# Computing the first chunk's hidden layer in two 256-row halves, with half of x transposed by the DMA

## The chip, the cores and the metric

The kernel runs on one core of a Trainium2 chip. The metric is the device time of one execution in microseconds (us); lower is better. The profile's span is about 1.8 us shorter than that time.

## The reference

Forward and backward of a two-layer block with SiLU in between, all in bfloat16; x and grad_out are 2048 x 640, w1 is 640 x 1536, w2 is 1536 x 640.

```python
def _fwd_reference(x, w1, w2):
    h = jnp.einsum("bsd,df->bsf", x, w1)
    h = _silu(h)
    out = jnp.einsum("bsf,fd->bsd", h, w2)
    return out
# reference: out, and the gradients of x, w1, w2 for a given grad_out
```

## The kernel before

The 2048 rows are processed in four chunks of 512. For a chunk the kernel computes h (w1 stationary, x transposed as moving operand), then the out product, then the gradients. The first chunk differs from the others: at the start nothing is loaded, so its x is transposed on TensorE, and h, the out product, the g matmuls and the gradient of x follow one another. All loads go into one DMA queue, in program order. While the first load is under way, 36 matmuls on zeros keep TensorE busy ("warm"), so that its clock comes up.

```python
        warm = cpool.tile([P, P], dt_in, name="warm")
        nc.vector.memset(warm[:], 0.0)
        warm_a = cpool.tile([P, 1], FP32, name="warm_a")
        nc.scalar.activation(warm_a[:], warm[:, 0:1], ACT.Silu)
        wp = ps_h.tile([P, SC], FP32, name="wp", tag="hp")
        for i in range(NWARM):
            nc.tensor.matmul(wp[:, 0:P], lhsT=warm[:], rhs=warm[:], start=True, stop=True)
        # ... identity, weight tiles, load_xT and load_goT (DMA transposes of 512 rows)

        def pe_xT(c, halves):
            xT = xpool.tile([P, DT, SC], dt_in, name="xT")
            nst = STC // halves
            for hh in range(halves):
                for dt_ in range(DT):
                    tp = ps_h.tile([P, nst, P], dt_in, name="tp", tag="hp")
                    for j in range(nst):
                        st = c * STC + hh * nst + j
                        nc.tensor.transpose(tp[:, j, :], x_nat[:, st, dt_ * P:(dt_ + 1) * P], ident[:])
                    dst = xT[:, dt_, hh * nst * P:(hh + 1) * nst * P]
                    if dt_ % 2 == 0:
                        nc.vector.tensor_copy(out=dst, in_=tp[:].rearrange("p j q -> p (j q)"))
                    else:
                        nc.scalar.copy(out=dst, in_=tp[:].rearrange("p j q -> p (j q)"))
            return xT

        FH = FC // 2
        nc.sync.dma_start(out=x_nat[:, 0:STC, :], in_=x_v[:, 0:STC, :])
        nc.sync.dma_start(out=w1_nat[:, :, 0:FH], in_=w1_v[:, :, 0:FH])
        nc.sync.dma_start(out=w1_nat[:, :, FH:FC], in_=w1_v[:, :, FH:FC])
        for fc in range(1, NFC):
            nc.sync.dma_start(out=w1_nat[:, :, fc * FC:(fc + 1) * FC], in_=w1_v[:, :, fc * FC:(fc + 1) * FC])
        for hf in range(2):
            nc.sync.dma_start(out=w2_nat[:, :, hf * DH:(hf + 1) * DH], in_=w2_v[:, :, hf * DH:(hf + 1) * DH])
        goT_next = load_goT(0)
        for fc in range(NFC):
            nc.sync.dma_start_transpose(out=w2T[:, :, fc * FC:(fc + 1) * FC], in_=w2[fc * FC:(fc + 1) * FC, :])
        nc.sync.dma_start_transpose(out=w1T[:], in_=w1[:, :])

        xT_next = pe_xT(0, 1)

        def h_group(ft, xT, aT, ghT):
            hp = ps_h.tile([P, SC], FP32, name="hp")
            for dt_ in range(DT):
                nc.tensor.matmul(
                    hp[:],
                    lhsT=w1_nat[:, dt_, ft * P:(ft + 1) * P],
                    rhs=xT[:, dt_, :],
                    start=(dt_ == 0),
                    stop=(dt_ == DT - 1),
                )
            nc.scalar.activation(aT[:, ft, :], hp[:], ACT.Silu)
            t = tpool.tile([P, SC], FP32, name="t")
            nc.scalar.activation(t[:], hp[:], ACT.Tanh, scale=0.5)
            v = tpool.tile([P, SC], dt_in, name="v")
            nc.vector.tensor_scalar(out=v[:], in0=t[:], scalar1=-0.5, scalar2=0.5, op0=ALU.mult, op1=ALU.add)
            nc.vector.scalar_tensor_tensor(
                out=ghT[:, ft, :], in0=aT[:, ft, :], scalar=1.0, in1=v[:], op0=ALU.subtract, op1=ALU.mult
            )

        # ... g_group: the same for grad_out and w2T

        def sd_phase(c, lhs_all, rhs_all, dst_v, on_act):
            o_sb = opool.tile([P, STC, D], dt_in, name="o_sb")
            for sl in range(STC):
                op_ = ps_o.tile([P, 2, 512], FP32, name="op")
                for ft in range(FT):
                    for hf in range(2):
                        nc.tensor.matmul(
                            op_[:, hf, 0:DH],
                            lhsT=lhs_all[:, ft, sl * P:(sl + 1) * P],
                            rhs=rhs_all[:, ft, hf * DH:(hf + 1) * DH],
                            start=(ft == 0),
                            stop=(ft == FT - 1),
                        )
                # ... copy out of PSUM, store

        for c in range(NCH):
            # ... next chunk's transposes
            if c == 0:
                for ft in range(FT):
                    h_group(ft, xT, aT, ghT)
                nc.sync.dma_start(
                    out=aT_scr[:, c * SC:(c + 1) * SC].rearrange("(ft p) s -> p ft s", p=P), in_=aT[:]
                )
                sd_phase(c, aT, w2_nat, out_v, True)
                for ft in range(FT):
                    g_group(ft, goT, ghT)
                # ... ghT to memory, gradient of x
                continue
            # ... chunks 1 to 3: h and g groups alternate
```

## Time and profile before

| | |
|---|---|
| time, first three runs (us) | 323.03 median, 323.01 to 323.51 |
| span of the profiled run | 321.2 |
| TensorE busy | 316.2 (98%) |
| first h matmul starts | 6.35 |
| first matmul of the out product starts | 19.30 |
| second half of w2 has landed | 18.60 |

Two parts of the page of the kernel before: its first line, and the chain of work that ended last, by engine.

```profile
span 321.2 us, 4386 instructions
...
## 4 chain that ended last, share of the span: by engine, by line
PE 97%; DMA 1%; issue 0%; DVE 0%; DVEq 0%
```

TensorE (PE) is nearly the whole chain. What it does not own is the head, which the timeline of TensorE shows. The columns are start and length in us, engine, line, operation, what it writes and reads, the shapes, the count, and in brackets the idle time before and what ended it.

```profile
0.99 3.81 PE L90 MATMUL wp<-warm 128*128 128x128 bf16 x36 [0.99 <-DVE warm L85]
5.06 1.30 PE L118 MATMUL tp<-ident,x_nat 128*128 128x128 bf16 x20 [0.26 <-DMA x_nat<-in_x_dram]
6.35 13.11 PE L144 MATMUL hp<-xT,w_nat 128*128 128x512 bf16 x58
19.30 13.20 PE L180 MATMUL op<-w_nat,aT 128*128 128x320 bf16 x96
```

The transposes begin when x has landed, h follows at once, the out product follows h at once. So this head is made of one wait (x) and then pure TensorE work: the 12.95 us from 6.35 to 19.30 are 60 matmuls at 216 ns (two of the 60 records are missing from the trace). To start h sooner is the only way to shorten it, and it pays only while nothing else becomes the last to arrive.

The same view of the queue that issues the loads:

```profile
0.74 0.43 SPq L127 DMA_DIRECT2D x_nat<-in_x_dram  x1
1.24 0.49 SPq L128 DMA_DIRECT2D w_nat<-in_w_dram  x1
1.77 0.52 SPq L129 DMA_DIRECT2D w_nat<-in_w_dram  x1
2.34 2.36 SPq L131 DMA_DIRECT2D w_nat<-in_w_dram  x2
4.74 4.92 SPq L133 DMA_DIRECT2D w_nat<-in_w_dram  x2
9.70 9.09 SPq L107 DMA_TRANSPOSE goT<-in_grad_out_dram  x1
```

L127 is x, L128 to L131 are the four pieces of w1, L133 the two halves of w2, L107 the first DMA transpose. These are issue times. When a load has landed is in the trace's landing records (the last of the load's 16 completions): x 5.01, w1's pieces 6.08, 7.15, 9.30 and 11.21, w2's halves 14.79 and 18.60. The out product uses both halves of w2 from its second matmul on, so w2 has 0.7 us of room: 18.60 against 19.30.

### The profile page before, as it was taken

The numbers are of one execution on the slowest core, as the hardware profiler recorded it, in microseconds if no ns is written. First come the engines' busy times: TensorE is split into PE (matmuls) and PEld (weight loads), VectorE is DVE, ScalarE is ACT, GpSimd is POOL, SyncE is SP. The second block draws the span as 40 slices with busy tenths as digits, with TensorE's granted clock in tenths as the row PEclk, the third lists the DMA queues.
The fourth block names the chain that finished last, engine by engine and source line by source line (L and its number), as shares of the span: only waits on it lengthen the run. The fifth ranks groups of instructions, "written<-read, shape, count | busy, mean of one in ns | idle before, by whom it ended". The sixth has DMA issues, their size and how long they took to land.

```text
span 321.2 us, 4386 instructions
## 1 busy us (share of the span) xinstructions
PE 316.2 (98%) x1926; PEld 188.5 (59%) x1944; DVE 99.1 (31%) x172; ACT 78.9 (25%) x136; POOL 0.7 (0%) x6
## 2 busy tenths in 40 slices
PE   8999999999999999999999999999999999999996
PEld 6467457544577644477754467777777775444443
DVE  1860553577501287800357740220000000110001
ACT  3961000455210155411044521001111111000100
POOL 0000000000000000000000000000000000000000
PEclk9999999999999999999999999999999999999999
DMA  7999999998794020291020079909999996211111
GB/s 235 318 191 200 220 274 241 363 289 274 213 290 137 6 78 0 78 316 67 17 82 0 0 254 245 239 17 236 226 218 213 266 219 211 85 38 44 35 42 41
DMA packets 113731, 52.32 MB, mean 163 GB/s; under 512 B 84144, under 2 KB 113712, under 8 KB 113712
## 3 DMA queue, kind: packets, MB, share of 16 engines
q1 hardware_dynamic: 113712, 52.04, 64.1%
q8 instruction: 15, 0.25, 0.3%
q14 instruction: 4, 0.03, 0.0%
HBM read 9.18 MB, written 21.76 MB: 96 GB/s over the span
## 4 chain that ended last, share of the span: by engine, by line
PE 97%; DMA 1%; issue 0%; DVE 0%; DVEq 0%
PE op L180 32%; PE op L263 16%; PE hp L163 16%; PE hp L144 16%; PE hp L302 15%; DMA x_nat<-in_x_dram 1%; PE hp L284 1%; PE tp L118 0%; DVE g_2755 L295 0%; DVEq L295 0%
## 5 line engine op out<-in xcount | busy, mean ns | idle before, releaser
L144 PE MATMUL hp<-xT,w_nat 128*128 128x512 bf16 x229 | 56.3, 379 | 0.6
L163 PE MATMUL hp<-goT,w2T 128*128 128x512 bf16 x238 | 56.8, 379 | 0.1
L180 PE MATMUL op<-w1T,ghT 128*128 128x320 bf16 x384 | 52.8, 299 | 0.0
L180 PE MATMUL op<-w_nat,aT 128*128 128x320 bf16 x384 | 52.8, 299 | 0.0
L263 PE MATMUL op<-go_nat,a_blk 128*128 128x320 bf16 x384 | 52.3, 299 | 0.0
L151 ACT ACTIVATE aT<-hp 128x512 bf16<-128x512 f32 x48 | 28.7, 597 | 83.0 <-PE hp L144 83.0
L302 PE MATMUL hp<-gh_blk,x_nat 128*128 128x512 bf16 x219 | 48.2, 379 | 0.3
L180 PEld LDWEIGHTS <-aT 128*128 128x128 bf16 x384 | 37.5, 98 | 15.3
L180 PEld LDWEIGHTS <-ghT 128*128 128x128 bf16 x384 | 37.5, 98 | 14.8
L263 PEld LDWEIGHTS <-a_blk 128*128 128x128 bf16 x384 | 37.5, 98 | 14.7
L163 PEld LDWEIGHTS <-w2T 128*128 128x128 bf16 x240 | 23.5, 98 | 28.2
L144 PEld LDWEIGHTS <-w_nat 128*128 128x128 bf16 x240 | 23.4, 98 | 27.8
L170 DVE SCALAR_TENSOR_TENSOR ghT<-ghT,hp 128x512 bf16<-128x512 bf16 x48 | 32.5, 682 | 16.2 <-PE hp L163 16.2
L191 DVE CAST o_sb<-op 128x640 bf16<-128x640 f32 x16 | 13.2, 825 | 78.6 <-PE op L180 78.6
L302 PEld LDWEIGHTS <-x_nat 128*128 128x128 bf16 x224 | 21.9, 98 | 26.3
L156 DVE SCALAR_TENSOR_TENSOR ghT<-aT,v 128x512 bf16<-128x512 bf16 x48 | 33.0, 687 | 0.6
L153 ACT ACTIVATE t<-hp 128x512 f32<-128x512 f32 x48 | 28.4, 592 | 0.0
L155 DVE TENSOR_SCALAR v<-t 128x512 bf16<-128x512 f32 x48 | 20.5, 427 | 20.5 <-ACT t L153 20.5
L189 ACT ACTIVATE o_sb<-op 128x640 bf16<-128x640 f32 x16 | 11.2, 703 | 49.1 <-PE op L180 49.1
L270 ACT ACTIVATE gw_sb<-op 128x640 bf16<-128x640 f32 x12 | 8.4, 704 | 56.8 <-PE op L263 56.8
L313 DVE CAST g_2475<-hp 128x512 bf16<-128x512 f32 x1 | 0.7, 690 | 58.2 <-PE hp L302 58.2
L90 PE MATMUL wp<-warm 128*128 128x128 bf16 x36 | 3.8, 304 | 1.0 <-DVE warm L85 1.0
(31 smaller groups left out, 26.2 us busy)
## 6 DMA issues: line engine op xcount, KB each, us to landing
aT_scr<-aT SPq DMA_DIRECT2D x4, 1536.0 KB, 6.3
ghT_scr<-ghT SPq DMA_DIRECT2D x4, 1536.0 KB, 9.6
out_dram<-o_sb SPq DMA_DIRECT2D x8, 640.0 KB, 4.4
x_nat<-in_x_dram SPq DMA_DIRECT2D x4, 640.0 KB, 5.4
go_nat<-in_grad_out_dram SPq DMA_DIRECT2D x4, 640.0 KB, 7.0
w_nat<-in_w_dram SPq DMA_DIRECT2D x2, 960.0 KB, 11.5
out_dram<-gw_sb SPq DMA_DIRECT2D x1, 1920.0 KB, 6.9
w_nat<-in_w_dram SPq DMA_DIRECT2D x2, 640.0 KB, 7.6
```

The lines of the kernel that those rows point to most:

```text
L144: nc.tensor.matmul(hp[:], lhsT=w1_nat[:, dt_, ft * P:(ft + 1) * P], rhs=xT[:, dt_, :], start=(dt_ == 0), stop=(dt_ == DT - 1),)
L151: nc.scalar.activation(aT[:, ft, :], hp[:], ACT.Silu)
L153: nc.scalar.activation(t[:], hp[:], ACT.Tanh, scale=0.5)
L155: nc.vector.tensor_scalar(out=v[:], in0=t[:], scalar1=-0.5, scalar2=0.5, op0=ALU.mult, op1=ALU.add)
L156: nc.vector.scalar_tensor_tensor(out=ghT[:, ft, :], in0=aT[:, ft, :], scalar=1.0, in1=v[:], op0=ALU.subtract, op1=ALU.mult)
L163: nc.tensor.matmul(gp[:], lhsT=w2T[:, dt_, ft * P:(ft + 1) * P], rhs=goT[:, dt_, :], start=(dt_ == 0), stop=(dt_ == DT - 1),)
L170: nc.vector.scalar_tensor_tensor(out=ghT[:, ft, :], in0=ghT[:, ft, :], scalar=1.0, in1=gp[:], op0=ALU.add, op1=ALU.mult)
L180: nc.tensor.matmul(op_[:, hf, 0:DH], lhsT=lhs_all[:, ft, sl * P:(sl + 1) * P], rhs=rhs_all[:, ft, hf * DH:(hf + 1) * DH], start=(ft == 0), ...
L189: nc.scalar.activation(dst, op_[:, :, 0:DH], ACT.Copy)
L191: nc.vector.tensor_copy(out=dst, in_=op_[:, :, 0:DH])
L263: nc.tensor.matmul(op_[:, hf, 0:DH], lhsT=a_blk[:, st, :], rhs=go_nat[:, st, hf * DH:(hf + 1) * DH], start=(st == 0), stop=(st == ST - 1),)
L302: nc.tensor.matmul(gp[:], lhsT=x_nat[:, st, dt_ * P:(dt_ + 1) * P], rhs=gh_blk[:, st, :], start=(st == 0), stop=(st == ST - 1),)
```

## The change

The intent is to start h sooner. Of the first 512 rows of x only 256 are loaded and transposed on TensorE; they come as two loads on two issuing engines. w1 comes in six pieces of 256 columns, so that the first piece follows quickly. h of the first chunk is computed in two halves of 256 rows, two blocks of 128 columns of w1 sharing a PSUM bank, so that the ScalarE and VectorE instructions behind it still handle 512 elements each. The second 256 rows come by a DMA transpose, queued behind w1 and ahead of w2. The warm matmuls go from 36 to 25 plus 4. The compiled order puts those 4 ahead of the transposes, so PE runs 29 of them at a stretch.

```diff
-    NWARM = 36
+    NWARM = 25
+    NFILL = 4
 ...
-        nc.sync.dma_start(out=x_nat[:, 0:STC, :], in_=x_v[:, 0:STC, :])
-        nc.sync.dma_start(out=w1_nat[:, :, 0:FH], in_=w1_v[:, :, 0:FH])
-        nc.sync.dma_start(out=w1_nat[:, :, FH:FC], in_=w1_v[:, :, FH:FC])
-        for fc in range(1, NFC):
-            nc.sync.dma_start(out=w1_nat[:, :, fc * FC:(fc + 1) * FC], in_=w1_v[:, :, fc * FC:(fc + 1) * FC])
+        XH = SC // 2
+        NXH = XH // P
+        xT_next = xpool.tile([P, DT, SC], dt_in, name="xT")
+        nc.sync.dma_start(out=x_nat[:, 0, :], in_=x_v[:, 0, :])
+        nc.scalar.dma_start(out=x_nat[:, 1, :], in_=x_v[:, 1, :])
+        for fp in range(F // XH):
+            nc.sync.dma_start(
+                out=w1_nat[:, :, fp * XH:(fp + 1) * XH], in_=w1_v[:, :, fp * XH:(fp + 1) * XH]
+            )
+        nc.scalar.activation(warm_a[:], warm[:, 0:1], ACT.Silu)
+        nc.sync.dma_start_transpose(out=xT_next[:, :, XH:SC], in_=x2[XH:SC, :])
         for hf in range(2):
             nc.sync.dma_start(out=w2_nat[:, :, hf * DH:(hf + 1) * DH], in_=w2_v[:, :, hf * DH:(hf + 1) * DH])
         goT_next = load_goT(0)
 ...
-        xT_next = pe_xT(0, 1)
+        DS = 3
+        for st in range(NXH):
+            tp = ps_o.tile([P, 2, 8, P], dt_in, name="tp", tag="op")
+            for dt_ in range(DT):
+                b, q = (0, dt_) if dt_ < DS else (1, dt_ - DS)
+                nc.tensor.transpose(tp[:, b, q, :], x_nat[:, st, dt_ * P:(dt_ + 1) * P], ident[:])
+            nc.vector.tensor_copy(out=xT_next[:, 0:DS, st * P:(st + 1) * P], in_=tp[:, 0, 0:DS, :])
+            nc.scalar.copy(out=xT_next[:, DS:DT, st * P:(st + 1) * P], in_=tp[:, 1, 0:DT - DS, :])
+        for i in range(NFILL):
+            nc.tensor.matmul(wp[:, 0:P], lhsT=warm[:], rhs=warm[:], start=True, stop=True)
 ...
+        def h_pair(ft, half, xT, aT, ghT):
+            lo, hi = half * XH, (half + 1) * XH
+            hp = ps_h.tile([P, SC], FP32, name="hp")
+            for g in range(2):
+                h_mm(hp[:, g * XH:(g + 1) * XH], ft + g, xT, lo, hi)
+            h_tail(hp[:].rearrange("p (g s) -> p g s", g=2), aT[:, ft:ft + 2, lo:hi], ghT[:, ft:ft + 2, lo:hi])
 ...
             if c == 0:
-                for ft in range(FT):
-                    h_group(ft, xT, aT, ghT)
+                for half in range(2):
+                    for ft in range(0, FT, 2):
+                        h_pair(ft, half, xT, aT, ghT)
```

(Cut: h_mm and h_tail, which hold h_group's matmuls and its four ScalarE and VectorE instructions, and the late load of the 256 rows of x that the weight gradient needs.)

More of the change, by code (lines that the diff above doesn't have):

```diff
@@ L86 @@
         warm_a = cpool.tile([P, 1], FP32, name="warm_a")
-        nc.scalar.activation(warm_a[:], warm[:, 0:1], ACT.Silu)
         wp = ps_h.tile([P, SC], FP32, name="wp", tag="hp")
@@ L108, in load_goT @@
             return goT
-        def pe_xT(c, halves):
-            xT = xpool.tile([P, DT, SC], dt_in, name="xT")
-            nst = STC // halves
-            for hh in range(halves):
-                for dt_ in range(DT):
-                    tp = ps_h.tile([P, nst, P], dt_in, name="tp", tag="hp")
-                    for j in range(nst):
-                        st = c * STC + hh * nst + j
-                        nc.tensor.transpose(tp[:, j, :], x_nat[:, st, dt_ * P:(dt_ + 1) * P], ident[:])
-                    dst = xT[:, dt_, hh * nst * P:(hh + 1) * nst * P]
-                    if dt_ % 2 == 0:
-                        nc.vector.tensor_copy(out=dst, in_=tp[:].rearrange("p j q -> p (j q)"))
-                    else:
-                        nc.scalar.copy(out=dst, in_=tp[:].rearrange("p j q -> p (j q)"))
-            return xT
-        FH = FC // 2
-        nc.sync.dma_start(out=x_nat[:, 0:STC, :], in_=x_v[:, 0:STC, :])
-        nc.sync.dma_start(out=w1_nat[:, :, 0:FH], in_=w1_v[:, :, 0:FH])
-        nc.sync.dma_start(out=w1_nat[:, :, FH:FC], in_=w1_v[:, :, FH:FC])
-        for fc in range(1, NFC):
-            nc.sync.dma_start(out=w1_nat[:, :, fc * FC:(fc + 1) * FC], in_=w1_v[:, :, fc * FC:(fc + 1) * FC])
+        XH = SC // 2
[9 more added lines that the diff above has]
+        nc.sync.dma_start_transpose(out=xT_next[:, :, XH:SC], in_=x2[XH:SC, :])
         for hf in range(2):
@@ L137, with h_tail, h_mm @@
         nc.sync.dma_start_transpose(out=w1T[:], in_=w1[:, :])
-        xT_next = pe_xT(0, 1)
-        def h_group(ft, xT, aT, ghT):
-            hp = ps_h.tile([P, SC], FP32, name="hp")
+        DS = 3
[8 more added lines that the diff above has]
+            nc.tensor.matmul(wp[:, 0:P], lhsT=warm[:], rhs=warm[:], start=True, stop=True)
+        def h_tail(hp, a_out, gh_out):
+            nc.scalar.activation(a_out, hp, ACT.Silu)
+            t = tpool.tile([P, SC], FP32, name="t")
+            nc.scalar.activation(t[:], hp, ACT.Tanh, scale=0.5)
+            v = tpool.tile([P, SC], dt_in, name="v")
+            nc.vector.tensor_scalar(out=v[:], in0=t[:], scalar1=-0.5, scalar2=0.5, op0=ALU.mult, op1=ALU.add)
+            vv = v[:] if len(a_out.shape) == 2 else v[:].rearrange("p (g s) -> p g s", g=a_out.shape[1])
+            nc.vector.scalar_tensor_tensor(
+                out=gh_out, in0=a_out, scalar=1.0, in1=vv, op0=ALU.subtract, op1=ALU.mult
+            )
+        def h_mm(hp, ft, xT, lo, hi):
             for dt_ in range(DT):
                 nc.tensor.matmul(
-                    hp[:],
+                    hp,
                     lhsT=w1_nat[:, dt_, ft * P:(ft + 1) * P],
-                    rhs=xT[:, dt_, :],
+                    rhs=xT[:, dt_, lo:hi],
                     start=(dt_ == 0),
@@ L150, in h_group @@
                 )
-            nc.scalar.activation(aT[:, ft, :], hp[:], ACT.Silu)
-            t = tpool.tile([P, SC], FP32, name="t")
-            nc.scalar.activation(t[:], hp[:], ACT.Tanh, scale=0.5)
-            v = tpool.tile([P, SC], dt_in, name="v")
-            nc.vector.tensor_scalar(out=v[:], in0=t[:], scalar1=-0.5, scalar2=0.5, op0=ALU.mult, op1=ALU.add)
-            nc.vector.scalar_tensor_tensor(
-                out=ghT[:, ft, :], in0=aT[:, ft, :], scalar=1.0, in1=v[:], op0=ALU.subtract, op1=ALU.mult
-            )
+        def h_group(ft, xT, aT, ghT):
+            hp = ps_h.tile([P, SC], FP32, name="hp")
+            h_mm(hp[:], ft, xT, 0, SC)
+            h_tail(hp[:], aT[:, ft, :], ghT[:, ft, :])
+        def h_pair(ft, half, xT, aT, ghT):
+            lo, hi = half * XH, (half + 1) * XH
+            hp = ps_h.tile([P, SC], FP32, name="hp")
+            for g in range(2):
+                h_mm(hp[:, g * XH:(g + 1) * XH], ft + g, xT, lo, hi)
+            h_tail(hp[:].rearrange("p (g s) -> p g s", g=2), aT[:, ft:ft + 2, lo:hi], ghT[:, ft:ft + 2, lo:hi])
         def g_group(ft, goT, ghT):
@@ L205 @@
             if c == 2:
+                nc.sync.dma_start(out=x_nat[:, NXH:STC, :], in_=x_v[:, NXH:STC, :])
                 for j in range(STC, ST, STC):
```

## The prediction

> **What bounds the kernel now.** TensorE: the page has PE busy 98% of a 321.2 us span and 97% of the chain that ended last. Only the head is decided by something else: the chain starts with 4.26 us of waiting for the load of x (issued 0.74, landed 5.01), then 20 transposes (5.06 to 6.35), then h. From the first h matmul (6.35, one 0.2 us gap) to the first matmul of the out product (19.30) PE runs a 512-column matmul every 216 ns (timeline). So the change can win only the head.
>
> **What it wins.** Before h, only 320 KB of x and 320 KB of w1 must land. In the packet records of before, 640 KB had moved by about 4.3 us, the slowest engine landing at 5.0. The 29 warm matmuls at 107 ns end near 4.1; ten transposes instead of twenty save 0.6; the copies end about 5.2. I expect the first h matmul at 5.2 to 5.3, 1.0 to 1.1 us earlier. The clock should be full by then: the Trainium skill ("TensorE: Matmul & The Clock Gate", Part 1) says about 3.4 us of activity lift it; this trace agrees: warm matmuls go from 107 to 55 ns apart at 4.3 us. 120 matmuls of 256 columns should take 108 ns each, 12.96 us like 60 of 512: transposes with a weight load each run 55 ns apart, so loads stay hidden. ACT and DVE instructions keep their 512 elements and cost.
>
> **What it adds, and why the win is lost.** Rows 256 to 511 now come by a DMA transpose queued behind all of w1, and w2 behind that.
> 1. Half 0 of h ends about 11.8 us (6 x 1.08). w1 at 290 to 310 KB/us (its 512-byte packets) is moved by about 9.8. In before the first DMA transpose (goT) began with a stall: its first packets, from 16.5 on, all ended at 18.4, when the last engine had finished w2. Engine spread at the end of w1 is 0.9 us (landings 10.3 to 11.2). So: wait to 10.7, 1.15 us of data (283 KB/us), 0.6 to landing: about 12.5; PE waits 0.7 us. The 16 KB instruction fetch at 15.2, near PE's 194th instruction, moves to about 11.4 and may delay one engine by 1 us more.
> 2. The out product needs both halves of w2; the second landed at 18.6, only 0.7 us ahead of its use. Now it follows a transpose that holds the queue about 2 us where 1 us of x is saved: about 19.6 (18.9 to 20.4). PE, done with h at 19 to 20, starts the out product at about 19.7 instead of 19.30.
> Later loads (goT landed 21.9, needed 32.5; w1T 40.3, needed 45.5) have room for 2 us.
>
> **Prediction.** The head's 1 us is handed back; net +0.4 us: 323.4 us, range 322.3 to 324.6. Chances: faster by over 2% 0.01, within 0.98, slower 0.01.
>
> **What will show it.** First h matmul near 5.25; 256-column matmuls 108 ns apart; a PE gap of 0.5 to 1.5 us between the halves, ended by the DMA of xT; w2's second half landing 18.9 to 20.4 with a PE wait before the out product; later phases unchanged (13.04 us per 96 out matmuls).
>
> **What would make it wrong.** xT landing by 11.8 and w2 by 18.3: then about 322.0. The clock lifted late because of the shorter warm-up: 1 to 3 us worse. w1 pieces falling behind PE.

## The result, and the profile after

The changed kernel took 323.76 us (median of 4 runs, 323.27 to 324.10); the kernel before, in the same rounds, 323.27 (323.01 to 323.70). The ratio is 1.0013, 95% interval 0.9992 to 1.0033: the same.

The page of the changed kernel, the same two parts:

```profile
span 321.5 us, 4496 instructions
...
## 4 chain that ended last, share of the span: by engine, by line
PE 93%; DMA 3%; SPq 3%; issue 0%; DVE 0%; DVEq 0%
```

TensorE has lost 4% of the chain to the DMA and to the queue that issues it (SPq, the queue of SyncE). The chain in order of time shows where (start, length, what):

```profile
5.76 3.52 SPq L120
9.28 0.05 issue
9.33 0.57 SPq L122
9.90 0.05 issue
9.95 9.70 DMA w_nat<-in_w_dram
19.64 0.04 issue
19.68 13.06 PE op L192 x95
```

Before 19.68 nothing of TensorE is in this chain. What ended last is the load of w2 (L122, its second half issued at 9.95), behind the DMA transpose (L120). It landed at 19.64, and the out product runs from 19.68. The issue was not what held it, though the chain passes through it: in the packet records w2's first packet starts at 11.21, as the transpose's last packets end (11.21 to 11.32). The timeline of TensorE:

```profile
0.99 2.85 PE L90 MATMUL wp<-warm 128*128 128x128 bf16 x25 [0.99 <-DVE warm L86]
3.63 0.63 PE L137 MATMUL wp<-warm 128*128 128x128 bf16 x4
4.06 1.27 PE L133 MATMUL tp<-ident,x_nat 128*128 128x128 bf16 x10
5.78 13.73 PE L152 MATMUL hp<-xT,w_nat 128*128 128x256 bf16 x120 [0.45 <-DVE xT L134]
19.34 13.40 PE L192 MATMUL op<-w_nat,aT 128*128 128x320 bf16 x96
```

h starts at 5.78 instead of 6.35, but it ends no sooner: 19.34 against 19.30. The out product's first matmul needs the first half of w2 only and runs at 19.34; the other 95 wait. So the shift of everything after is 0.25 us (the g matmuls can start at 32.75 instead of 32.50), and the span is 0.27 us longer.

Two causes compete for the lost microsecond. **Theory W**: w2 lands a microsecond later, by the prediction because it now stands behind a DMA transpose, so it bounds the head wherever TensorE is. **Theory C**: the head's win was lost on TensorE itself. In this trace the clock was raised late, at 6.77 us (in the profile of before at 4.43). The groups of TensorE instructions between 3.9 and 6.3 us, with busy time and mean ns of one, first before, then after:

```profile
L118 PE MATMUL tp<-ident,x_nat 128*128 128x128 bf16 x20 | 1.3, 220 | 0.3 <-DMA x_nat<-in_x_dram 0.3
```

```profile
L133 PE MATMUL tp<-ident,x_nat 128*128 128x128 bf16 x10 | 1.3, 314 | 0.0
L152 PE MATMUL hp<-xT,w_nat 128*128 128x256 bf16 x3 | 0.8, 405 | 0.4 <-DVE xT L134 0.4
```

A transpose took 314 ns for 220; they started 107 ns apart for 55. Ten transposes cost 0.5 us more, and the first five h matmuls, which took 1.0 us (0.6 in a later run with a full clock), 0.4 us more. That is about the missing microsecond on TensorE, so theory C is a serious one. The Trainium skill ("TensorE: Matmul & The Clock Gate", Part 1) says the clock is raised after a busy window of about 3.4 us, and that the window runs freely, whatever the kernel's start. If so, a late clock is a matter of the run, not of the kernel; after_again and before_w2ft below bear that out.

### The profile page after: what moved, and what is told of

Read it like the earlier page. It is cut to its first block, busy times and chain, and to the rows that moved or that the text cites. A ratio compares the mean times of both kernels' runs of the same rounds, so it can differ in the third digit from the quotient of the medians.

```text
span 321.5 us, 4496 instructions
## 1 busy us (share of the span) xinstructions
PE 317.2 (99%) x1987; PEld 194.3 (60%) x1987; DVE 98.7 (31%) x171; ACT 78.7 (24%) x136; POOL 0.7 (0%) x6
## 4 chain that ended last, share of the span: by engine, by line
PE 93%; DMA 3%; SPq 3%; issue 0%; DVE 0%; DVEq 0%
PE op L192 32%; PE op L277 16%; PE hp L175 16%; PE hp L316 15%; PE hp L152 12%; DMA w_nat<-in_w_dram 3%; SPq L116 1%; SPq L120 1%; PE hp L298 1%; SPq L122 0%; SPq L113 0%; DVE g_2799 L309 0%; DVEq L309 0%
## 5 line engine op out<-in xcount | busy, mean ns | idle before, releaser
L152 PE MATMUL hp<-xT,w_nat 128*128 128x512 bf16 (+1 forms) x300 | 57.5, 339 | 0.4 <-DVE xT L134 0.4
L152 PEld LDWEIGHTS <-w_nat 128*128 128x128 bf16 x300 | 29.6, 99 | 22.9 <-issue 0.6
L90 PE MATMUL wp<-warm 128*128 128x128 bf16 x25 | 2.8, 313 | 1.0 <-DVE warm L86 1.0
```

Of the source, the lines that this page charges most:

```text
L152: nc.tensor.matmul(hp, lhsT=w1_nat[:, dt_, ft * P:(ft + 1) * P], rhs=xT[:, dt_, lo:hi], start=(dt_ == 0), stop=(dt_ == DT - 1),)
```

## The experiments

Ten runs were made after these two: seven further kernels, and three repeats. The table has what all twelve profiles show of the head, in us. "Clock up" is the granted clock's first rise in the records; "h done" is the start of the first out matmul, or, where that had to wait for w2 too, 109 ns after the last h matmul's start; "out runs" is from when the out product runs without a break.

| kernel | clock up | first h | h done | w2 landed (1st, 2nd) | out runs | span |
|---|---|---|---|---|---|---|
| before | 4.43 | 6.35 | 19.30 | 14.79, 18.60 | 19.30 | 321.2 |
| changed | 6.77 | 5.78 | 19.34 | 16.88, 19.64 | 19.68 | 321.5 |
| after_again | 4.62 | 5.50 | 18.71 | 17.09, 19.84 | 19.88 | 321.7 |
| after_w2ft | 5.05 | 5.71 | 18.88 | 15.77, 18.45 | 18.88 | 320.8 |
| after_w2ft_b | 3.94 | 5.17 | 18.35 | 16.01, 18.66 | 18.35 | 320.3 |
| after_w2q | 4.91 | 5.64 | 19.03 | last of four: 20.04 | 19.03 | 320.9 |
| before_w2ft | not recorded, about 6.8 by the spacing | 7.03 | 19.98 | 13.71, 16.38 | 19.98 | 321.9 |
| before_extraT | 4.07 | 6.35 | 19.30 | 15.77, 19.78 | 19.83 | 321.7 |
| after_extraT | 3.86 | 5.14 | 18.73 | 19.61, 22.35 | 22.39 | 324.1 |
| after_peT | not recorded, before 3.9 by the spacing | 5.03 | 20.20 | 15.95, 19.20 | 20.20 | 322.2 |
| after_peT_b | not recorded, about 4.1 by the spacing | 5.22 | 20.40 | 16.12, 19.17 | 20.40 | 322.4 |
| before_halves | 4.87 | 6.41 | 20.61 | 15.12, 18.67 | 20.61 | 322.5 |

### after_again: the changed kernel, unaltered

> The changed kernel once more, unaltered, to see what varies. In its first profile the clock came up at 6.77 us (in before at 4.43), so transposes and five h matmuls ran at half rate and h ended at 19.34; w2's second half landed at 19.64 and ended the last wait of the head. Theory W (w2's landing bounds the head): w2 again lands at 19.3 to 20.0 and the out product runs from there, whatever the clock does; with an early clock h ends near 18.4 and PE then waits about 1.2 us. Theory C (the late clock ate the win): with an early clock the out product starts near 18.4 and the time is about 322.2.

Measured: 323.47 us (5 runs, 323.00 to 323.52); ratio to before 1.0006 (0.9993 to 1.0018). The clock came up early, at 4.62. The timeline of TensorE:

```profile
4.05 1.00 PE L133 MATMUL tp<-ident,x_nat 128*128 128x128 bf16 x10
5.50 13.38 PE L152 MATMUL hp<-xT,w_nat 128*128 128x256 bf16 x120 [0.45 <-DVE xT L134]
18.71 0.30 PE L192 MATMUL op<-w_nat,aT 128*128 128x320 bf16 x1
19.88 13.06 PE L192 MATMUL op<-w_nat,aT 128*128 128x320 bf16 x95 [0.87 <-DMA w_nat<-in_w_dram]
```

h ended 0.63 us sooner than in the first profile, and it bought nothing: one out matmul at 18.71, then 1.17 us to the next, ended by w2. The span was even 0.2 us longer, because w2 landed 0.2 us later. As the only cause of the loss, theory C falls: the clock moved h, not the time.

### after_w2ft: the changed kernel, w2 in row halves

```diff
-        for hf in range(2):
-            nc.sync.dma_start(out=w2_nat[:, :, hf * DH:(hf + 1) * DH], in_=w2_v[:, :, hf * DH:(hf + 1) * DH])
+        for q in range(2):
+            nc.sync.dma_start(out=w2_nat[:, q * FT // 2:(q + 1) * FT // 2, :], in_=w2_v[:, q * FT // 2:(q + 1) * FT // 2, :])
```

> The changed kernel with w2 loaded in two halves by rows of F (first six row blocks, then six) instead of two halves by columns of D. The out product then needs the second half only after 12 of its matmuls (1.6 us). Theory W: the wait before the out product goes; it starts as soon as h ends (18.4 with an early clock, 19.3 with a late one), so the time falls by 0.3 us with a late clock and by about 1.3 us with an early one, to about 322.2 to 323.2. Theory C: only the 0.3 us with a late clock, nothing more with an early one.

Measured: 322.87 us (322.19 to 323.19); ratio to before 0.9987 (0.9974 to 0.9999); 0.6 us under the changed kernel's median of the same rounds. The wait is gone: h done and out product both at 18.88. The first half of w2 was there at 15.77. The second landed at 18.45, sooner than 19.84, which has to do with its rows: packets of 1280 bytes where there were 640. From its first packet to its last, w2 took 6.8 us here (11.0 to 17.8) and 7.9 us in after_again (11.4 to 19.3). So two things changed at once, which after_w2q takes apart.

### before_w2ft: the same edit in the kernel before

> The kernel before with the same edit of w2's load. Its w2 landed 0.7 us ahead of its use, so no wait is there to take away: both theories expect the same time as before within 0.2 us. If it is faster, the new shape of the load does something else than end the wait.

Measured: 323.36 us (323.15 to 323.68); ratio 1.0007 (0.9994 to 1.0020): the same. w2 was complete at 16.38, 2.2 us sooner than in the kernel before, and no time came of it, as nobody waited for it. The profile of this run also fell on a late clock: its transposes ran 107 ns apart until 6.8 and h was done at 19.98 instead of 19.30. A late clock costs the kernel before 0.7 us, in span as well (321.9 for 321.2). So the clock does matter wherever TensorE is what bounds the head; in the changed kernel the wait for w2 hid it.

### before_extraT: one more DMA transpose ahead of w2, in the kernel before

```diff
+        xdum = wpool.tile([P, DT, 256], dt_in, name="xdum")
+        nc.sync.dma_start_transpose(out=xdum[:], in_=x2[256:512, :])
         for hf in range(2):
             nc.sync.dma_start(out=w2_nat[:, :, hf * DH:(hf + 1) * DH], in_=w2_v[:, :, hf * DH:(hf + 1) * DH])
```

> The kernel before with one more DMA transpose of rows 256 to 511 of x, into a tile that nobody reads, put ahead of w2's loads. Nothing changes on PE. Theory W: w2's second half lands about 2 us later (20 to 21 instead of 18.6), the out product starts there instead of at 19.30, and the time rises by 1.0 to 1.5 us, to about 324.4. Theory C: no change, as TensorE and its clock see nothing of it.

Measured: 323.57 us (4 runs, 323.48 to 324.70); ratio 1.0023 (1.0006 to 1.0040). The direction is W's; the size was missed. w2 landed at 19.78, 1.2 us later and not 2, and of this 0.7 us was room. The rest is in the timeline of TensorE:

```profile
6.35 13.11 PE L146 MATMUL hp<-xT,w_nat 128*128 128x512 bf16 x58
19.30 0.30 PE L182 MATMUL op<-w_nat,aT 128*128 128x320 bf16 x1
19.83 13.06 PE L182 MATMUL op<-w_nat,aT 128*128 128x320 bf16 x95 [0.23 <-DMA w_nat<-in_w_dram]
```

The wait before the out product is that of the changed kernel. But here the transpose comes on top of the same loads, while in the changed kernel it stands in place of 320 KB of plain load. So the 1.2 us are the price of one more transpose, and not yet an account of the changed kernel's 1.0 us. The out product's break shifts the g matmuls from 32.50 to 32.89, and the span is 0.5 us longer.

### after_extraT: one more, in the changed kernel

The same edit, with rows 512 to 767 as its data, behind the transpose that the change put there.

> The suspected cost doubled: the changed kernel with one more 256-row DMA transpose into a tile that nobody reads, put ahead of w2's loads. In the kernel before the same addition moved w2's second landing by 1.2 us (18.6 to 19.8), of which 0.7 us of slack swallowed most. The changed kernel has no slack left there, so theory W expects w2 at about 21.0, the out product from there, and the time up by 1.0 to 1.3 us on the changed kernel, to about 324.6. Theory C expects no change.

Measured: 325.26 us (4 runs, 324.57 to 327.53, an unusual spread); ratio 1.0075 (1.0036 to 1.0113). The timeline of TensorE:

```profile
5.14 13.75 PE L154 MATMUL hp<-xT,w_nat 128*128 128x256 bf16 x120 [0.45 <-DVE xT L136]
19.65 0.30 PE L194 MATMUL op<-w_nat,aT 128*128 128x320 bf16 x1 [0.76 <-DMA w_nat<-in_w_dram]
22.39 11.84 PE L194 MATMUL op<-w_nat,aT 128*128 128x320 bf16 x86 [2.45 <-DMA w_nat<-in_w_dram]
```

With no room left, the delay of w2 comes through whole: the second half landed at 22.35, 2.5 us after that of after_again, and the span is 2.4 us longer. The dose in this profile was twice what was expected. The second transpose landed 2.7 us after the first (14.73 and 12.01), for 320 KB that would take 1.13 us at the 283 KB/us at which transposes stream here.

The packet records show that this is not the price of a transpose behind a transpose. The second one followed the first without a stall, and 30 of the 32 small packets that report its completion were written by 12.67, 1.1 us after those of the first. But its last 26 data packets ended one by one from 13.32 to 14.02. From 12.35 to 13.29 one packet of 16,384 bytes from the instruction queue was under way; most likely it kept one of the 16 DMA engines busy (which engine a packet is on is not recorded). The copies of w2 that had started behind the transpose from 12.6 on ended only at 14.1. So about 1.4 us of the 2.5 are an accident of timing. Two of the four runs, without a trace, took 324.57 and 324.60, which is the 324.6 that was expected.

### after_peT: the second 256 rows transposed on TensorE

The changed kernel without its DMA transpose: rows 256 to 511 by a plain load ahead of w1's fifth piece, ten transposes on TensorE before the fifth pair of half 0.

```diff
-        nc.sync.dma_start_transpose(out=xT_next[:, :, XH:SC], in_=x2[XH:SC, :])
+            if fp == F // XH - 2:      # in the loop of w1's pieces
+                nc.sync.dma_start(out=x_nat[:, NXH:STC, :], in_=x_v[:, NXH:STC, :])
 ...
+                        if half == 0 and ft == FT - 4:
+                            for st in range(NXH, STC):
+                                # five transposes into a tile of ps_h, one VectorE copy to xT
```

> One part of the change undone: rows 256 to 511 of x come by a plain load (ahead of the last two pieces of w1) and are transposed on TensorE inside half 0 of h, ten transposes, as in the kernel before; the two halves, the small pieces and the early start stay. Theory W: without the transpose in the queue w2's second half lands about 1.1 us sooner, at 18.6 to 18.8; PE pays 0.56 us for ten transposes and perhaps 0.4 us for the later pieces of w1, ends h at 19.3 to 19.7 and then waits for nothing; time about that of the kernel before, 323.0 to 323.4. If the DMA transpose is not what holds w2 back, w2 still lands at 19.7.

Measured: 323.76 us (323.51 to 324.02); ratio 1.0019 (1.0007 to 1.0032). Half a hit. w2's first packet came 1.1 us sooner (its end at 10.2, for 11.2 and 11.4 in the two profiles of the changed kernel), which is what the transpose had held up. But w2 landed at 19.20, only 0.4 to 0.6 us sooner. Some DMA engine was behind the others from the third piece of w1 on (completions 6.51 to 8.21, for 6.69 to 7.44 in the changed kernel's first profile) and stayed so. And h was done at 20.20, 0.5 to 0.9 us later than expected; one wait inside h for that third piece took 0.96 us. Since h ended after w2, the run says nothing of W's price in time. The waits, in the timeline of TensorE:

```profile
8.25 2.37 PE L155 MATMUL hp<-xT,w_nat 128*128 128x256 bf16 x20 [0.80 <-DMA w_nat<-in_w_dram]
20.20 13.20 PE L195 MATMUL op<-w_nat,aT 128*128 128x320 bf16 x96
```

### after_peT_b: the same once more

> The run with rows 256 to 511 transposed on TensorE once more, because in its profile one DMA engine fell a microsecond behind from the second piece of w1 on and stayed behind: w2's first packet ended 1.1 us sooner than in the changed kernel, its last only 0.5 us. If that lag is chance, pieces land about 1 us apart here and w2's second half at 18.6 to 19.0; if it comes again, near 19.2. Either way h should end later than w2 lands and the time be 323.2 to 323.9.

(In that profile it was the third piece from which on an engine lagged, not the second.)

Measured: 324.19 us (4 runs, 324.09 to 324.20); ratio 1.0032 (1.0017 to 1.0047), just above what was expected. The lag came again, now from the second piece (5.42 to 7.26), w2 landed at 19.17, h was done at 20.40. So it is no chance of one run. Where transposes stand in the queue, the records show the engines brought level before they go on (last section); without one, a laggard keeps its lag to the end of w2. That the missing levelling is why w2 gained half of its 1.1 us fits the records, but no run isolates it, and which engine lags is not in the trace.

Both runs show one thing more. They load the same bytes ahead of w2's end as the kernel before, all as plain copies, and yet w2 lands at 19.20 and 19.17 instead of 18.60. The laggard alone does not make this: the first of w2's 16 completions was written at 16.55 and 16.50, in the kernel before at 16.06. So 0.5 to 0.6 us of delay are there without any transpose.

### after_w2q: row halves, but 640-byte packets

```diff
+        for q in range(2):
+            for hf in range(2):
+                fs, ds = slice(q * FT // 2, (q + 1) * FT // 2), slice(hf * DH, (hf + 1) * DH)
+                nc.sync.dma_start(out=w2_nat[:, fs, ds], in_=w2_v[:, fs, ds])
```

> The earlier run with w2 in row halves did two things: it let the out product start on the first half, and its longer rows (1280 bytes for 640) made w2 land at 18.45 instead of 19.8. Here only the first: w2 in four loads, row halves first, each cut by columns of D, so the packets stay at 640 bytes. Theory W: the last landing stays at 19.5 to 20, but it is needed only 1.6 us after the out product starts, at about 20.3 with an early clock, so the wait goes all the same and the time is that of the row-half version, 322.4 to 323.0. If only the faster rows had helped, it is that of the changed kernel, about 323.5.

Measured: 322.66 us (322.51 to 322.99); ratio 0.9985 (0.9973 to 0.9998). The last quarter landed at 20.04, later than in the changed kernel, and still there was no wait: the out product ran from 19.03 and needs the last two quarters 12 matmuls of 136 ns, 1.6 us, after its start.

```profile
5.64 13.56 PE L154 MATMUL hp<-xT,w_nat 128*128 128x256 bf16 x120 [0.45 <-DVE xT L136]
19.03 13.20 PE L194 MATMUL op<-w_nat,aT 128*128 128x320 bf16 x96
```

So the later deadline alone frees the win; the faster rows are not needed for it.

### after_w2ft_b: the best version once more

> The changed kernel with w2 in row halves once more, to see whether its lead over the kernel before (0.9987) stands: theory W expects 0.998 to 0.9995, with no PE wait before the out product, and the rest of the spread from when the clock comes up (h ends 18.7 with an early clock, 19.3 with a late one).

Measured: 322.76 us (322.07 to 323.13); ratio 0.9987 (0.9974 to 0.9999), the same as the first time. The profile fell on the earliest clock of the row-half versions (3.94) and shows the head as it was meant:

```profile
3.62 0.54 PE L137 MATMUL wp<-warm 128*128 128x128 bf16 x4
4.00 0.72 PE L133 MATMUL tp<-ident,x_nat 128*128 128x128 bf16 x10
5.17 13.34 PE L152 MATMUL hp<-xT,w_nat 128*128 128x256 bf16 x120 [0.45 <-DVE xT L134]
18.35 13.20 PE L192 MATMUL op<-w_nat,aT 128*128 128x320 bf16 x96
```

The out product starts at 18.35, 0.95 us before that of the kernel before, and the span is 0.93 us shorter.

### before_halves: the halves alone

The kernel before with its loads and transposes, but h of the first chunk in h_pair's two halves.

> One part of the change alone: the kernel before with its loads and its twenty transposes as they are, but h of the first chunk in two halves of 256 rows, 120 matmuls of 256 columns. From the changed kernel's trace such a matmul takes 109.2 ns, so 120 of them cost 0.15 us more than 60 of 216 ns. The halves also read all of w1 in half the time: the third to sixth pair need the 512-column pieces that landed at 9.3 and 11.2 us, at about 8.7 and 11.5, so PE should wait about 0.6 us once. h should end at about 20.0 instead of 19.30, and the time rise by about 0.7 us to 323.9. If the halves were free by themselves, h ends at 19.3 to 19.5 and the time is the same.

Measured: 323.84 us (323.77 to 324.31); ratio 1.0024 (1.0012 to 1.0037). The size in time came out, the place did not. PE waited 1.07 us more than a matmul's spacing, once, and after only three h matmuls (6.63 to 7.80). The wait ended with w1's second piece, which landed at 7.76 (in the first profile at 7.15) and which only the second pair reads; so in the compiled order matmuls of the second pair must stand ahead of the rest of the first. By estimate, with the pairs in order the second would have waited from 7.50 to 7.76 and the third from 8.85 to 9.64, when its piece landed, about as much in all. h was done at 20.61, 1.3 us later. The matmuls themselves cost what was computed, 109.2 ns each.

## Why the prediction was right

The time, 323.76 us in a range of 322.3 to 324.6 around 323.4, was right, and so was the place where the win is lost: the wait for w2. The sum that put w2 there was right by luck in part, as two of its terms were off by about as much. Point by point:

- **w2, item 2: right in the result, mis-sized in both terms.** Predicted about 19.6 (18.9 to 20.4), measured 19.64 and 19.84. Predicted start of the out product about 19.7, measured 19.68 and 19.88. That w2 is what bounds the head is shown by making its deadline later at the same packets (after_w2q), which alone brings the time under that of before. That a transpose ahead of w2 delays it is shown by adding one (before_extraT). But the sum was "about 2 us" for the transpose less "1 us" for the x that is not loaded. The first term was smaller: w2 landed 1.2 us later in before_extraT, and from w1's last landing to w2's it took 8.92 us in the changed kernel, 7.39 before, which is 1.5 us more. The second was smaller too: w1's last piece landed at 10.72 instead of 11.21, so only 0.5 us of the saving reached w2. 1.5 less 0.5 makes the same 1.0 us.
- **What ate the saving: not isolated, most likely w1's smaller pieces.** Cut to 256 columns, all of w1 comes in packets of 512 bytes, where its last 1,280 KB had come in packets of 1,024. From 7 to 8 and from 8 to 9 us the DMA moved 355 and 359 GB/s in the kernel before, 291 and 292 in the changed one. These 1,280 KB took 3.8 to 4.1 us from landing to landing in the four profiles with wide pieces, 4.3 to 4.7 in the six with narrow ones and a transpose behind them. Going by the 0.6 us that after_peT keeps without a transpose, about half of w2's microsecond is the transpose's and half comes with the rest of the change; this is an estimate. The kernel before with w1 in six pieces would have tested it; it was not run.
- **First h matmul, 5.2 to 5.3: right with an early clock only.** With the clock up by 4.0 us it was 5.03 to 5.17 (after_peT, after_extraT, after_w2ft_b). In the two profiles of the changed kernel the clock came at 6.77 and 4.62 and h at 5.78 and 5.50. The step that failed is "the clock should be full by then": it was read from one trace. The change moves ten transposes and the first h matmuls to 4 to 6 us, which is where the clock comes up; in the kernel before, waiting for x until 5.06, they mostly came after it. This did not show in the time of the changed kernel because w2 hid it.
- **PE wait for the second half of x, 0.7 us: wrong, there was none.** I put its landing at 12.5 and the end of half 0 at 11.8. It landed at 11.86 and 12.03. The stall came as predicted (its packets were let go at 10.57, predicted 10.7), and the 0.54 us from the last packet (11.32) to the landing (11.86) were close to the 0.6 predicted. The term that was mis-sized is the data after the stall: 530 of the transpose's 1,280 packets had gone ahead or were under way by then, so 0.66 us were left and not 1.15. The trace of before could have told: of the transpose behind w2, 503 packets ended before its stall did. Even with an early clock no gap opened (after_w2ft_b: landed at 11.57). The instruction fetch came at 12.96, 12.32 and 11.68, after that landing, and did no harm there.
- **256-column matmuls, 108 ns: slightly low.** They are 109.2 ns apart. The Trainium skill ("TensorE: Matmul & The Clock Gate", "Wait — 56ns, not 53.3ns?") gives a fixed cost of about 2.5 ns per matmul on a full clock; twice 109.2 less 215.8 is 2.6, so this trace agrees. 120 matmuls instead of 60 cost 0.15 us.
- **Later phases unchanged: right.** The 95 out matmuls left take 13.06 us, like those of before (13.04 for 96, by the chain).

So of the 1.0 to 1.1 us at the head, 0.95 was really there (after_w2ft_b), less with a later clock. The changed kernel gave it back and ended 0.3 to 0.5 us behind: in after_again all at the wait for w2; in the first profile the late clock had already taken the win, and w2 took 0.3 us more. The version with w2 in row halves keeps about half of it on average: 0.13% under the kernel before in both tries, each time with an upper bound just under 1.

What stays open: why two of the changed kernel's first four runs took 324.0 to 324.1 us, as they have no trace; how w2's delay divides between the transpose and w1's smaller packets; and why a DMA engine fell behind early in w1 in both runs of after_peT.

## What to carry to other kernels

Before bringing a critical load forward, write down the room that each later load in the same queue has: here w2 had 0.7 us, and a win of 1 us at the head needed 0.3 us that it did not have. If a matmul loop accumulates over a dimension, cut its operand's load along that dimension, in the order of use; the loop can then start on the first part, and the deadline of the rest moves back by the work on the first. A DMA transpose in a queue of copies can cost those behind it more than the copy that it replaces (here w2 landed 0.4 to 0.7 us later than with plain loads), so place it behind the loads that have no room. And when a load is cut into narrower pieces so that the first comes sooner, look at what the shorter packets do to everything behind it.

## What the Trainium skill lacked or had wrong

- "DMA: Bandwidth & Descriptors", "DMA Transpose (X-bar)": it has no word on what a transpose does to the queue at its start and its end. In the kernel before, 503 packets of the transpose behind w2 had ended by 18.4, but some twenty that had started from 16.5 us on ended only at 18.4, when the last engine had done with w2 (18.14); and w2's completions, of which 15 of 16 were written by 17.0, landed together at 18.51 to 18.60. At the other end, in after_extraT, copies that had started from 12.6 on ended at 14.1, after the transpose's last packet (14.02). One 256-row transpose (320 KB) added behind w1 delayed w2 by 1.2 us.
- The same page, "Latency and other measured facts", gives 261 GB/s as a transpose's effective bandwidth where the middle dimension is not contiguous. While streaming, the transposes here moved 283 KB/us (290 GB/s); from first packet to last, stall included, the 320 KB of the changed kernel took 1.88 us (9.44 to 11.32), 174 GB/s.
- "TensorE: Matmul & The Clock Gate", "What you observe", has the clock come up around 4 us into matmul activity, 500 ns more or less from run to run. Nine profiles of nearly the same head had it between 3.86 and 6.77 us after the span's start, 2.9 to 5.8 us after the first matmul (0.99). Its 500 ns are too narrow; it cost up to 0.7 us here. Its free-running window of 3413 ns fits: in all nine the clock stayed up for a whole number of such windows (92, 93 or 94).
- No page has a number for what an instruction fetch costs the loads beside it. In the kernel before there are 15, each one packet of 16,384 bytes, 0.9 to 1.4 us long. One ran from 15.18 to 16.29, and the last of w2's 16 completions was written 1.14 us after the 15th (18.14 and 17.00). In before_w2ft, where it began at 15.48 with w2 nearly done, that lag was 0.08 us. So w2's small room of 0.7 us is itself likely the work of one such fetch; as the records do not name the engine of a packet, this is inferred.
